# A gated mix of linear attention and a gated MLP on one core: first down weights loaded ahead of the gate weights, another order of low parts and gated additions at the end

## The chip, the cores and the metric

The kernel runs on one core of a Trainium2 chip. The metric is the device time of one execution in microseconds (us). Engines: PE multiplies matrices into PSUM, DVE and POOL do elementwise work, ACT does activations and copies, SP issues most DMAs. Each works through its own instructions in order, and waits on semaphores where it needs another's result.

## The reference

With `x` of 2048 tokens by 576:

```python
g = _sigmoid((x * gate_w).sum(-1, keepdims=True))
a = _A_ref(x, A_wqkv, A_wo)          # linear attention, 32 heads of 18, then @ wo
b = _B_ref(x, B_w_gate, B_w_up, B_w_down)
return g * a + (1 - g) * b
# _B_ref:
h = _gelu(x @ w_gate) * (x @ w_up)   # 576 -> 4608
return h @ w_down                    # 4608 -> 576
```

Everything is float32.

## The kernel before, in words

A float32 factor is split into a high part, which PE takes in one pass (`F32R`), and a low part, which is the rest; a product is three matmuls (high by high, high by low, low by high). ACT copies the high part, and DVE or POOL subtracts it for the low part.

The attention part comes first (lines 98 to 752). What is used of it here: `r2` holds the query features of one block of 512 tokens; `kw` holds the weights of the mixing product (`mixed`, L716), whose results, scaled by `g`, go to DRAM as `ga_d`. Its last `rb` loads are issued by SP at L695.

The MLP works in 36 periods. Each takes 256 of the 4608 features for one half of the tokens (1024); 18 periods do the first half, 18 the second. All products of a period are done by a scheme with seven half-size products for a 2 x 2 block product (`PRODUCTS`, L36), so sums of blocks are formed ahead (`S1` to `S4` of the left factor, `T1` to `T4` of the weights) and results are combined behind.

- Gate and up products `G1` to `G7`, `U1` to `U7` (`product`, L767): seven matmuls of 512 columns each, into four PSUM banks `bk`. DVE combines them (`gu2`, `ge3`, `uu2` and so on, all through the helper at L794), ACT applies the gelu (`gel0` to `gel3`, L791) in the tiles `e0` to `e3`; `um0` to `um3` make the four blocks of `h`.
- Down products `D20` to `D71` (`unit`, L870) of the period before, in 14 half units of six matmuls of 288 columns, into two PSUM pairs `pr`. DVE adds each (`E20` to `E71`, L879) to `sums`, which holds one half of the output.
- The left factors: `h11`, `h12`, `h22` and the sums `S1` to `S4`, each with a high copy on ACT (names in h, L917) and a low part on DVE or POOL (names in l, L918). `s1`, `s2`, `s3`, `s4` form the sums themselves; `S3` is made from `s3` alone. They lie in the tiles `h0` to `h3` and `hx0` to `hx2`.
- Down weights: `dld` loads `draw` (576 KB, L936); `dsT1` to `dsT4` form the sums in `dsum` on POOL and DVE; `dhr` and `dht` copy high parts to `wd` on ACT; `dlr0`, `dlr1`, `dlt0`, `dlt1` are low parts (L942). Gate and up weights of the first half go the same way from `work` (`wld0`, `wld1`, then `ws...`, `whr`, `wlr`, `wht`, `wlt`) to `wg` and `wu`; the second half loads them ready-made.

The order of a period's steps is written out by hand in `ORDER` (L38): it is recorded step by step by `emit`, and each engine's queue is what falls to it from that list. `@` puts a step on POOL instead of DVE, `+1` makes it belong to the period before. `tables` holds variants for three periods; that of the last, `LAST`, moves four steps ahead of `D10` and turns the order of the down products (what stands as `D10` becomes `D70`, which reads `S3`).

All tiles of the MLP are placed one behind the other in one pool, over tiles of the attention part that are done by then. A tile waits for the last instructions that used the memory beneath it. Before, `draw` begins in the memory of `kw`, with `dsum` behind it, and `e1` to `e3` lie in that of `r2`.

After the last period there are only its own down products. `parts(i)` (L1074) copies the high part of block `i` of `h` on ACT and notes its low part; `low_parts` (L1069) records the noted ones on DVE, one call later. `last_weights` (L1080) splits the last down weights, with two low parts on POOL (L1083). `down` (L1087) computes 128 tokens at a time, twelve matmuls a tile; `down_out` multiplies by `1 - g` and adds the sums (L1104, or by column halves at L1102), and SP stores the tile. Ahead of that, each tile of `sums` is scaled by `1 - g` on ACT and `ga_d`'s rows, loaded to `work` and `xu`, are added on POOL (`gated`, L863); for tiles whose sums are complete it is recorded behind the `G` and `U` steps.

Of the kernel before, what the change touches and what calls it, by code (L numbers as in the profile page):

```python
# [8 lines left out]
F32 = mybir.dt.float32  # L9
# [7 lines left out]
NB, BS = 4, 512  # L17
# [32 lines left out]
def tile_gated_mix(ctx, tc, xt, xr, xs, wkv, wvt, wq, wo, wgu, wgt, wdn, cst, out):  # L50
    nc = tc.nc
# [14 lines left out]
    def f32(ap):  # L66
        return ap.bitcast(F32)
# [479 lines left out]
    turn = Scope()  # L547
# [230 lines left out]
    es = [e0]  # L778
    add, sub, mul = OP.add, OP.subtract, OP.mult
# [4 lines left out]
    def ps(m, role):  # L784
        return bk[PLACE[m][role]]

    def copy(o, i):
        nc.scalar.activation(o, i, AF.Copy)  # L788
# [4 lines left out]
    def tt(o, a, b, op):  # L793
        nc.vector.tensor_tensor(o, a, b, op)  # L794
# [8 lines left out]
    def first_after(k):  # L803
# [6 lines left out]
        else:  # L810
# [15 lines left out]
    mp = mlp.pool("mp")  # L826
    work = mp.tile([128, 4 * 1024], F32, name="work")
    wraw, tsum = ([work[:, i * 1024:(i + 1) * 1024].rearrange("p (i k c) -> p i k c", i=4, k=2) for i in r]
                  for r in ((0, 1), (2, 3)))
    draw, dsum = (mp.tile([128, 4, 288], F32, name=x) for x in ("draw", "dsum"))  # L830
    es += [mp.tile([128, BS], F32, name=f"e{i}") for i in range(1, 4)]
    hs = [mp.tile([128, 2, BS], F32R, name=f"h{i}") for i in range(4)]
    hx = [mp.tile([128, 2, BS], F32R, name=f"hx{i}") for i in range(3)]
    hb = {A11: hs[0], A12: hs[1], A22: hs[3], S3: hs[2], S1: hx[0], S2: hx[1], S4: hx[2]}
# [5 lines left out]
    LAST = NQD - 1  # L840
# [4 lines left out]
    def feature(n):  # L845
        return n if n < NF2 else LAST - n

    def mix_of(t):
        return work[:, t * D:(t + 1) * D] if t < 7 else xu.rearrange("p a c -> p (a c)")[:, :D]
# [4 lines left out]
    def halves(t):  # L854
        return t.rearrange("p (n c) -> p n c", n=2)

    def acc_of(t):
        return sums[:, 0:2, t] if t < 4 else sums[:, 2:4, t - 4]

    def out_of(st):  # L860
        return halves(out[st * 128:(st + 1) * 128, :])

    def gated(p, t):  # L863
        st, m = p * PER + t, halves(mix_of(t))
        nc.scalar.activation(acc_of(t), acc_of(t), AF.Copy, scale=gate[:, 1, st:st + 1])
        nc.gpsimd.tensor_tensor(acc_of(t) if p else m, acc_of(t), m, add)
        if p == 0:
            nc.sync.dma_start(out_of(st), m)

    def unit(k, q):  # L870
# [67 lines left out]
    for x, i, src in (("r", slice(0, 3), draw[:, 1:4]), ("t", slice(3, 7), dsum)):  # L938
        op(f"dh{x}", lambda n, e, i=i, src=src: copy(wd[:, i, 0], src))
        for j in range(2):  # L940
            c = slice(j * 144, (j + 1) * 144)
# [8 lines left out]
    def w_load(n, m):  # L950
        nc.sync.dma_start(f32(W[m]), wp_d[feature(n)][m])

    for m in range(2):
# [6 lines left out]
        for j in range(2):  # L960
            i, o = slice(2 * j, 2 * j + 2), slice(3 + 2 * j, 5 + 2 * j)
# [35 lines left out]
    def valid(name, n):  # L997
        if name[0] == "w":
            return 1 <= n < NF2 - name.startswith("wst")
        if name[0] == "x":  # L1000
            return 2 <= n < 14
        if name[0] == "d":
            return 0 <= n < LAST and n != NF2
        return 0 <= n < LAST + (name[0] in "GUgu")
# [8 lines left out]
    def before(t, a, b):  # L1013
        w = [x for x in t if x[0] == a][0]
        t = [x for x in t if x[0] != a]
        t.insert([x[0] for x in t].index(b), w)
        return t
# [1 line left out]
    turned = {1: "7", 6: "4", 5: "1", 3: "6", 7: "5", 4: "3", 2: "2"}  # L1019
    tables = {0: before(table, "U4", "U3"), NF2: before(table, "G4", "G2")}  # L1020
    last = table
    for name in ("dlt0", "dlt1", "S3h", "S3l"):
        last = before(last, name, "D10")
    tables[LAST] = [(x[0] + turned[int(x[1])] + x[2:], s, e) if x[0] in "DE" and s == 1 else (x, s, e)
                    for x, s, e in last]
    last_of = [[name for name, _, _ in table if name[0] == g][-1] for g in "GU"]
# [4 lines left out]
    after = deque()  # L1031

    def emit(name, n, e):
        if (name, n) in done or not valid(name, n):
            return
        assert not (after and name[0] == "E" and n % NF2 == 0 and CHAINS[int(name[1])][1] in (C21, C22))
        done.add((name, n))
        ops[name](n, e)
        if name[0] in "GU":
            if after:  # L1040
                gated(*after.popleft())
            if n == NF2 - 1 and name[0] == "U":
                a = PRODUCTS[int(name[1])][0]
                nc.sync.dma_start(f32(xo[:, a]), xop_d[:, a])
            m = "GU".index(name[0])
            if name == last_of[m] and NF2 <= n < LAST:
                w_load(n + 1, m)
        if n in (NF2 - 1, LAST - 1):
            for t in range(PER):
                key = (n // NF2, t)  # L1050
                if key not in called and all((f"E{k}{t % 4 // 2}", n) in done for k in ENDS[t // 4]):
                    called.add(key)
                    after.append(key)

    for m in range(2):
        emit(f"wld{m}", 1, None)
    for p in range(-1, LAST):
        if p == LAST - 1:
            for t in range(PER):
                mix_load(1, t)  # L1060
        if p == NF2:
            for t in range(PER):
                mix_load(0, t)
        for name, shift, e in tables.get(p, table):
            emit(name, p - shift, e)

    lows = []

    def low_parts():  # L1069
        for i, src in lows:  # L1070
            tt(hs[i][:, 1], src, f32(hs[i][:, 0]), sub)
        lows.clear()

    def parts(i):  # L1074
        low_parts()
        src = es[i] if i in (0, 3) else ps(1, "d" if i == 1 else "e")
        copy(hs[i][:, 0], src)
        lows.append((i, src))

    def last_weights():  # L1080
        copy(wd[:, :4, 0], draw)
        for c in (slice(0, 144), slice(144, 288)):
            nc.gpsimd.tensor_tensor(wd[:, :4, 1, c], draw[:, :, c], f32(wd[:, :4, 0, c]), sub)  # L1083

    place = {}

    def down(t, f, turn, by_halves):  # L1087
        if f == 1:
            place[t] = ([ps(1, "c")[:, :288], ps(1, "a")[:, :288]] if t == 6 else
                        [pr[turn % 2][:, i, :288] for i in range(2)])  # L1090
        y = place[t]
        h, c = hs[(0 if t < 4 else 2) + f], slice((t % 4) * 128, (t % 4 + 1) * 128)
        for k, (a, wl) in enumerate(((0, 0), (0, 1), (1, 0))):
            for i in range(2):
                nc.tensor.matmul(y[i], h[:, a, c], wd[:, (1 - i, 2 + i)[f], wl], start=f == 1 and k == 0,  # L1095
                                 stop=f == 0 and k == 2, skip_group_check=True)

    def down_out(t, turn, by_halves):
        a, st, y = acc_of(t), PER + t, place[t]
        if t == 6 or by_halves:  # L1100
            for i in range(2):
                nc.vector.scalar_tensor_tensor(a[:, i], y[i], gate[:, 1, st:st + 1], a[:, i], op0=mul, op1=add)  # L1102
        else:
            nc.vector.scalar_tensor_tensor(a, pr[turn % 2][:, :, :288], gate[:, 1, st:st + 1], a, op0=mul, op1=add)  # L1104
        if by_halves:
            for i in range(2):
                nc.sync.dma_start(out_of(st)[:, i], a[:, i])
        else:
            nc.sync.dma_start(out_of(st), a)

    left = {name for name, _, _ in table if name[0] in "dD" and (name, LAST - 1) not in done}
    for p in (LAST, LAST + 1):
        for name, shift, e in tables.get(p, table):
            n = p - shift
            fresh = (name, n) not in done
            emit(name, n, e)
            if n == LAST and name in ("um0", "um1", "um2", "um3") and fresh:
                parts(int(name[2]))
            if n == LAST - 1 and name in left:
                left.discard(name)  # L1120
                if name[0] == "d" and not any(x[0] == "d" for x in left):
                    nc.sync.dma_start(draw, wdn[feature(LAST)])
                if not left:
                    last_weights()
    order = (0, 1, 2, 3, 4, 5, 6, 7) if last_of[1] in ("U4", "U7") else (4, 5, 6, 7, 0, 1, 2, 3)
    turns = {t: k - (k > order.index(6)) for k, t in enumerate(order)}
    low_parts()
    while after:
        gated(*after.popleft())
    for group in (order[:2],) + tuple((t,) for t in order[2:]):  # L1130
        for f in (1, 0):
            for t in group:
                down(t, f, turns[t], t == order[-1])
        for t in group:
            down_out(t, turns[t], t == order[-1])
    mlp.close()
    base.close()
    fixed.close()
# [60 lines left out]
```

## Time and profile before

| | |
|---|---|
| median of 3 runs | 1505.3 us (1504.97 to 1505.55) |
| the profiled execution | 1505.87 us, of which its span from the first to the last instruction 1504.1 us |
| PE busy | 1488.0 us (99%) |
| DVE, POOL, ACT busy | 1126.8, 758.5, 580.2 us |
| mean granted clock of PE | 0.999 |

A timeline row shows the start in us from the span's start, the duration in us, the engine and line, the operation, the tiles it writes and reads, the count of merged instructions, and in brackets how long the engine had been idle and what ended that. Matmuls overlap, and their ends are modelled, so a row of matmuls is best read by the distance from its start to the next row's start. A row of the chain of waits shows start, duration and what held the chain in that time.

### The profile page before, as it was taken

What the parts mean: (1) busy time and instruction counts of PE and PEld (TensorE: products, weight loads), DVE (VectorE), ACT (ScalarE), POOL (GpSimd) and SP (SyncE); (2) the same over time, 40 slices, a digit from 0 to 9 for tenths busy, and PEclk for the clock granted to TensorE, in tenths of its full rate; (3) what the DMA queues carried; (4) which work ended last, traced back from release to release, by engine and by line L of the source; (5) the groups of instructions that cost most, each with busy time, mean ns of one, the idle gap of its engine ahead of it and who ended that gap; (6) DMA issues with size and microseconds to landing.
All of it is one profiled execution on the core that took longest, in us unless ns stands there. A gap on an engine that the chain in (4) does not pass through costs nothing.

```text
span 1504.1 us, 21831 instructions
## 1 busy us (share of the span) xinstructions
PE 1488.0 (99%) x8332; PEld 1320.2 (88%) x8332; DVE 1126.8 (75%) x1722; ACT 580.2 (39%) x952; POOL 758.5 (50%) x716
## 2 busy tenths in 40 slices
PE   8999999999999999999999999999999999999998
PEld 7999889888888888888888888888888888888887
DVE  6675676488878888888788777776777777777766
ACT  6676755334334433434333323323222222222223
POOL 3763312377887787887776634323322323323323
PEclk9999999999999999999999999999999999999999
DMA  6898537556677667666666385444333433444531
GB/s 201 275 350 308 152 124 228 184 195 222 242 250 242 217 213 239 208 203 236 231 230 210 89 347 183 147 179 166 139 139 146 180 151 139 153 182 157 200 139 63
DMA packets 118582, 295.60 MB, mean 197 GB/s; under 512 B 7181, under 2 KB 87245, under 8 KB 108110
## 3 DMA queue, kind: packets, MB, share of 16 engines
q1 hardware_dynamic: 114730, 281.04, 53.1%
q10 hardware_dynamic: 3380, 10.78, 2.0%
q0 software_dynamic: 368, 2.39, 0.5%
q8 instruction: 65, 1.06, 0.3%
q14 instruction: 39, 0.32, 0.1%
HBM read 181.51 MB, written 112.68 MB: 196 GB/s over the span
## 4 chain that ended last, share of the span: by engine, by line
PE 92%; POOL 2%; DMA 2%; DVE 1%; issue 1%; ACT 1%; SPq 1%; DVEq 0%; POOLq 0%
PE bank L775 52%; PE pair L876 26%; PE pair L716 4%; PE bank L483 3%; PE kp L218 2%; PE ms L259 1%; PE mp L259 1%; PE bank L486 1%; PE pair L1095 1%; PE den L658 1%; POOL work L934 1%; DMA row_raw<-xr 0%; DMA draw<-wdn 0%; DMA raw<-wgu 0%; DMA xr<-xt 0%
## 5 line engine op out<-in xcount | busy, mean ns | idle before, releaser
L794 DVE TENSOR_TENSOR sums<-pair,sums 128x576 f32<-128x576 f32 x474 | 354.8, 755 | 163.9 <-PE pair L876 152.1
L775 PE MATMUL bank<-xo,wg 128*128 128x512 f32 x1764 | 441.1, 393 | 1.2 <-POOL wg L962 1.2
L775 PE MATMUL bank<-xo,wu 128*128 128x512 f32 x1764 | 430.4, 393 | 1.0 <-DVE spare L794 1.0
L775 PEld LDWEIGHTS bank<-xo,wu 128*128 128x128 f32 x1764 | 323.6, 188 | 64.7 <-DVE spare L794 1.6
L775 PEld LDWEIGHTS bank<-xo,wg 128*128 128x128 f32 x1764 | 322.7, 189 | 60.4 <-POOL wg L962 1.9
L876 PEld LDWEIGHTS pair<-wd,h 128*128 128x128 f32 x1680 | 248.4, 189 | 20.0 <-ACT h L788 1.6
L876 PE MATMUL pair<-wd,h 128*128 128x288 f32 x1680 | 259.9, 297 | 2.0 <-ACT h L788 1.2
L794 DVE TENSOR_TENSOR spare<-bank,spare 128x512 f32<-128x512 f32 x216 | 148.3, 687 | 84.6 <-PE bank L775 69.2
L876 PEld LDWEIGHTS pair<-wd,hx 128*128 128x128 f32 x1260 | 179.1, 189 | 9.6 <-POOL hx L918 0.3
L876 PE MATMUL pair<-wd,hx 128*128 128x288 f32 x1260 | 184.7, 295 | 0.1
L788 ACT ACTIVATE spare<-bank 128x512 f32<-128x512 f32 x72 | 43.2, 600 | 353.5 <-PE bank L775 353.5
L918 POOL TENSOR_TENSOR h<-e,h 128x512 fp32r<-128x512 f32 x70 | 96.9, 1384 | 146.7 <-ACT h L788 146.7
L942 POOL TENSOR_TENSOR wd<-draw,wd 128x432 fp32r<-128x432 f32 x68 | 75.1, 1125 | 189.4 <-ACT wd L788 189.4
L934 POOL TENSOR_TENSOR work<-work 128x256 f32<-128x256 f32 x136 | 114.8, 854 | 5.3
L788 ACT ACTIVATE h<-e 128x512 fp32r<-128x512 f32 x71 | 44.4, 625 | 170.3 <-DVE e L794 170.3
L918 POOL TENSOR_TENSOR hx<-spare,hx 128x512 fp32r<-128x512 f32 x35 | 45.8, 1309 | 109.1 <-ACT hx L788 109.1
L794 DVE TENSOR_TENSOR e<-bank,spare 128x512 f32<-128x512 f32 x107 | 73.2, 684 | 8.2 <-PE bank L775 6.9
L788 ACT ACTIVATE wd<-draw 128x864 fp32r<-128x864 f32 (+1 forms) x35 | 32.7, 934 | 113.0 <-PE pair L876 110.5
L791 ACT ACTIVATE e<-e 128x512 f32<-128x512 f32 x108 | 65.5, 622 | 0.1
L942 POOL TENSOR_TENSOR wd<-dsum,wd 128x576 fp32r<-128x576 f32 x34 | 49.3, 1451 | 24.5 <-ACT wd L788 24.5
L716 PEld LDWEIGHTS pair<-kw,p 128*128 128x128 f32 x448 | 60.5, 189 | 0.7
L716 PE MATMUL pair<-kw,p 128*128 128x288 f32 x448 | 60.9, 295 | 0.0
(200 smaller groups left out, 1898.3 us busy)
## 6 DMA issues: line engine op xcount, KB each, us to landing
wg<-wp_d SPq DMA_DIRECT2D x17, 2240.0 KB
wu<-wp_d SPq DMA_DIRECT2D x17, 2240.0 KB
wp_d<-wg SPq DMA_DIRECT2D x16, 2240.0 KB
wp_d<-wu SPq DMA_DIRECT2D x16, 2240.0 KB
draw<-wdn SPq DMA_DIRECT2D x35, 576.0 KB
work<-wgu SPq DMA_DIRECT2D x34, 512.0 KB
xo<-xop_d SPq DMA_DIRECT2D x7, 1280.0 KB
wt_d<-tail_op SPq DMA_DIRECT2D x15, 448.0 KB
```

The source lines that it names most:

```text
L218: nc.tensor.matmul(ps[c][:, :n], xa, kvw[i][:rows, r, lo:lo + n], start=(k == 0), stop=(k == 13))
L259: nc.tensor.matmul(o, a, p[:, w, lo:lo + n], start=(t == 0 and i == 0 and first), stop=(t == NST - 1 and i == len(ops) - 1), skip_group_ch ...
L483: nc.tensor.matmul(ps, qw[i][:rows, c:c + 128], xa, start=(k == 0), stop=(k == 13))
L716: nc.tensor.matmul(y[:, i, :288], pa, w[:, i * 288:(i + 1) * 288], start=(n == 0), stop=(n == 13))
L775: nc.tensor.matmul(ps, w_, x_, start=start and i == 0, stop=i == 6, skip_group_check=not start)
L788: nc.scalar.activation(o, i, AF.Copy)
L791: nc.scalar.activation(o, i, AF.Gelu_apprx_tanh)
L794: nc.vector.tensor_tensor(o, a, b, op)
L876: nc.tensor.matmul(pr[q][:, j, :288], h[:, hl, c], wd[:, b, wl], start=start and i == 0, stop=i == 2, skip_group_check=not start)
L918: op(name + "l", lambda n, e, a=a, f=src_of: e.tensor_tensor(hb[a][:, 1], f(), f32(hb[a][:, 0]), sub))
L934: op(f"{name}T{i + 1}", lambda n, e, o=o, a=a, b=b: e.tensor_tensor(o, a, b, sub))
L942: op(f"dl{x}{j}", lambda n, e, i=i, src=src, c=c: e.tensor_tensor(wd[:, i, 1, c], src[:, :, c], f32(wd[:, i, 0, c]), sub))
```

## The change

It has five parts.

1. `dld` of period 0 is recorded ahead of `wld0` and `wld1`. For this the tiles `e1` to `e3` are placed ahead of `draw`, with a filler `gap` of 512 bytes a partition behind them: `draw` now begins where `r2` begins, and `e1` to `e3` lie over `kw`. All tiles behind lie 512 bytes further.
2. In the last period `S3h` moves ahead of `s1`; `S3l` and `dlt0` move ahead of `s2`, and `S3l` from POOL to DVE; `dlt1` stays at its place in `ORDER`.
3. Behind the last period's `um2` the low part of block 3 goes to POOL; the low parts of blocks 2, 1 and 0 follow on DVE, in this order, after `um0`.
4. `gated` of the second half of the tokens only notes its POOL addition in `added`; those noted are recorded behind the low part of block 3, the others after the last low parts. No `gated` is recorded behind the very last `U` product.
5. The last tiles are done in the order 6, 7, 4, 5, 0, 1, 2, 3, not 4, 5, 6, 7, 0, 1, 2, 3; the third goes to the two single banks. The last does all six matmuls of its first 288 columns, then those of the second, each in a bank of its own.

SP at the start of the loop, before (`rb` belongs to the attention part, `wgu` holds the raw gate and up weights, `wt_d` a part of the split ones):

```order
L695 DMA rb_2907<-rden_d11_66 128x1x256 x4
L695 DMA rb_2907<-rden_d11_66 64x1x256 x2
L955 DMA work_3270<-wgu 128x4x256 x2
L936 DMA draw_3271<-wdn 128x1152
L947 DMA wg_2874<-wt_d0_126 96x7x128
```

and after:

```order
L695 DMA rb_2907<-rden_d11_66 128x1x256 x4
L695 DMA rb_2907<-rden_d11_66 64x1x256 x2
L941 DMA draw_3275<-wdn 128x1152
L960 DMA work_3270<-wgu 128x4x256 x2
L952 DMA wg_2874<-wt_d0_126 96x7x128
```

The load of `draw` has passed the two loads of `work`. It waits for ACT's and DVE's last reading of `r2`; the first load of `work` waits for the last matmul on `kw`, as before.

DVE in the last period, before (`e2` holds `s3`; `e3` becomes `s1`, `spare` `s2`, `e1` `s4`; the rows of `sums` are `E20` and `E21`):

```order
L794 TENSOR_TENSOR e3_3275<-bank_3261,e3_3275 128x512
L794 TENSOR_TENSOR sums_3284<-pair_3265,sums_3284 128x576
L921 TENSOR_TENSOR spare_1924<-e3_3275,spare_1924 128x512
L794 TENSOR_TENSOR e1_3273<-bank_3264,spare_1924 128x512
L942 TENSOR_TENSOR wd_3283<-dsum_3272,wd_3283 128x4x144
L794 TENSOR_TENSOR sums_3284<-pair_3266,sums_3284 128x576
```

and after:

```order
L794 TENSOR_TENSOR e3_3273<-bank_3261,e3_3273 128x512
L794 TENSOR_TENSOR sums_3285<-pair_3265,sums_3285 128x576
L923 TENSOR_TENSOR h2_3279<-e2_3272,h2_3279 128x512
L947 TENSOR_TENSOR wd_3284<-dsum_3276,wd_3284 128x4x144
L926 TENSOR_TENSOR spare_1924<-e3_3273,spare_1924 128x512
L794 TENSOR_TENSOR e1_3271<-bank_3264,spare_1924 128x512
L794 TENSOR_TENSOR sums_3285<-pair_3266,sums_3285 128x576
```

The low part `S3l` (into `h2`) is new on DVE, and `dlt0` has passed `s2` and `s4`. On ACT the copy `h2<-e2` has passed the copies `hx0<-e3` and `spare<-bank`.

DVE after the last `U` products, before (bank 3264 is block 1 of `h`, bank 3261 block 2, `e3` block 3, `spare` block 0):

```order
L794 TENSOR_TENSOR bank_3264<-bank_3264,e1_3273 128x512
L794 TENSOR_TENSOR h3_3279<-e3_3275,h3_3279 128x512
L794 TENSOR_TENSOR bank_3261<-spare_1924,bank_3261 128x512
L794 TENSOR_TENSOR bank_3261<-bank_3261,e2_3274 128x512
L794 TENSOR_TENSOR h1_3277<-bank_3264,h1_3277 128x512
L794 TENSOR_TENSOR spare_1924<-bank_3263,spare_1924 128x512
L794 TENSOR_TENSOR h2_3278<-bank_3261,h2_3278 128x512
L794 TENSOR_TENSOR h0_3276<-spare_1924,h0_3276 128x512
```

and after:

```order
L794 TENSOR_TENSOR bank_3264<-bank_3264,e1_3271 128x512
L794 TENSOR_TENSOR bank_3261<-spare_1924,bank_3261 128x512
L794 TENSOR_TENSOR bank_3261<-bank_3261,e2_3272 128x512
L794 TENSOR_TENSOR spare_1924<-bank_3263,spare_1924 128x512
L1076 TENSOR_TENSOR h2_3279<-bank_3261,h2_3279 128x512
L1076 TENSOR_TENSOR h1_3278<-bank_3264,h1_3278 128x512
L1076 TENSOR_TENSOR h0_3277<-spare_1924,h0_3277 128x512
```

The low part into `h3` is gone from DVE; on POOL it stands behind the two low parts of the last weights and ahead of the eight additions into `sums`. The other three stand behind all sums.

The diff, without the layout lines told above and without `lows.clear()` and what it replaces:

```diff
@@ gated
+    added = deque()
+
     def gated(p, t):
         st, m = p * PER + t, halves(mix_of(t))
         nc.scalar.activation(acc_of(t), acc_of(t), AF.Copy, scale=gate[:, 1, st:st + 1])
-        nc.gpsimd.tensor_tensor(acc_of(t) if p else m, acc_of(t), m, add)
-        if p == 0:
+        if p:
+            added.append(lambda: nc.gpsimd.tensor_tensor(acc_of(t), acc_of(t), m, add))
+        else:
+            nc.gpsimd.tensor_tensor(m, acc_of(t), m, add)
             nc.sync.dma_start(out_of(st), m)
@@ tables
-    for name in ("dlt0", "dlt1", "S3h", "S3l"):
-        last = before(last, name, "D10")
+    for name, at in (("S3h", "s1"), ("S3l", "s2"), ("dlt0", "s2")):
+        last = before(last, name, at)
+    last = [(x, s, nc.vector if x == "S3l" else e) for x, s, e in last]
@@ emit
-            if after:
+            if after and (n < LAST or name != last_of[1]):
                 gated(*after.popleft())
@@ the loop's start
-    for m in range(2):
-        emit(f"wld{m}", 1, None)
+    for name, n in (("dld", 0), ("wld0", 1), ("wld1", 1)):
+        emit(name, n, None)
@@ the last period
                 parts(int(name[2]))
+                if name == "um2":
+                    low_part(*lows.pop(0), nc.gpsimd)
+                    while added:
+                        added.popleft()()
@@ the end
-    order = (0, 1, 2, 3, 4, 5, 6, 7) if last_of[1] in ("U4", "U7") else (4, 5, 6, 7, 0, 1, 2, 3)
+    order = (6, 7, 4, 5, 0, 1, 2, 3)
-    low_parts()
+    for i, src in sorted(lows, reverse=True):
+        low_part(i, src, nc.vector)
     while after:
         gated(*after.popleft())
-    for group in (order[:2],) + tuple((t,) for t in order[2:]):
+    while added:
+        added.popleft()()
+    for group in (order[:2],) + tuple((t,) for t in order[2:-1]):
...
+    for i in range(2):
+        for f in (1, 0):
+            down(order[-1], f, 0, True, (i,))
+    down_out(order[-1], 0, True)
```

More of the change, by code (lines that the diff above doesn't have):

```diff
@@ L829, in tile_gated_mix @@
                   for r in ((0, 1), (2, 3)))
+    es += [mp.tile([128, BS], F32, name=f"e{i}") for i in range(1, 4)]
+    mp.tile([128, 128], F32, name="gap")
     draw, dsum = (mp.tile([128, 4, 288], F32, name=x) for x in ("draw", "dsum"))
-    es += [mp.tile([128, BS], F32, name=f"e{i}") for i in range(1, 4)]
     hs = [mp.tile([128, 2, BS], F32R, name=f"h{i}") for i in range(4)]
@@ L1067, in tile_gated_mix, with low_part @@
     lows = []
[L1069 to L1072, printed above, removed]
+    def low_part(i, src, e):
+        e.tensor_tensor(hs[i][:, 1], src, f32(hs[i][:, 0]), sub)
     def parts(i):
-        low_parts()
         src = es[i] if i in (0, 3) else ps(1, "d" if i == 1 else "e")
@@ L1085, in tile_gated_mix, with down @@
     place = {}
-    def down(t, f, turn, by_halves):
+    def down(t, f, turn, by_halves, halves_too=(0, 1)):
         if f == 1:
-            place[t] = ([ps(1, "c")[:, :288], ps(1, "a")[:, :288]] if t == 6 else
+            place[t] = ([ps(1, "c")[:, :288], ps(1, "a")[:, :288]] if t == order[2] or by_halves else
                         [pr[turn % 2][:, i, :288] for i in range(2)])
@@ L1093, in down @@
         for k, (a, wl) in enumerate(((0, 0), (0, 1), (1, 0))):
-            for i in range(2):
+            for i in halves_too:
                 nc.tensor.matmul(y[i], h[:, a, c], wd[:, (1 - i, 2 + i)[f], wl], start=f == 1 and k == 0,
@@ L1099, in down_out @@
         a, st, y = acc_of(t), PER + t, place[t]
-        if t == 6 or by_halves:
+        if t == order[2] or by_halves:
             for i in range(2):
@@ L1124, in tile_gated_mix @@
                     last_weights()
-    order = (0, 1, 2, 3, 4, 5, 6, 7) if last_of[1] in ("U4", "U7") else (4, 5, 6, 7, 0, 1, 2, 3)
-    turns = {t: k - (k > order.index(6)) for k, t in enumerate(order)}
-    low_parts()
+    order = (6, 7, 4, 5, 0, 1, 2, 3)
+    turns = {t: k - (k > 2) for k, t in enumerate(order)}
+    for i, src in sorted(lows, reverse=True):
+        low_part(i, src, nc.vector)
     while after:
         gated(*after.popleft())
-    for group in (order[:2],) + tuple((t,) for t in order[2:]):
+    while added:
+        added.popleft()()
+    for group in (order[:2],) + tuple((t,) for t in order[2:-1]):
         for f in (1, 0):
             for t in group:
-                down(t, f, turns[t], t == order[-1])
+                down(t, f, turns[t], False)
         for t in group:
-            down_out(t, turns[t], t == order[-1])
+            down_out(t, turns[t], False)
+    for i in range(2):
+        for f in (1, 0):
+            down(order[-1], f, 0, True, (i,))
+    down_out(order[-1], 0, True)
     mlp.close()
```

## The prediction

> **What bounds the kernel now.** The chain of waits came first; it gives PE's pace.
>
> ```profile
> 327.51 1.59 PE pair L876 x12
> 329.10 6.45 PE bank L775 x28
> ```
>
> Undisturbed, 28 matmuls of 512 columns take 6.45 us, 0.230 each, and 12 of 288 columns 1.59, 0.1325 each. PE is on almost the whole chain, so the time falls only where its matmuls start later than this pace. Inside the loop PE keeps it; the timeline shows three places where it doesn't: the start of the loop, the last period, the end. First the start.
>
> ```profile
> 286.95 5.15 PE L775 MATMUL bank<-xo,wu 128*128 128x512 f32 x21
> 293.14 5.09 PE L775 MATMUL bank<-xo,wu 128*128 128x512 f32 x21 [1.04 <-DVE spare L794]
> 298.07 0.63 PE L775 MATMUL bank<-xo,wg 128*128 128x512 f32 x2
> ```
> ```profile
> 312.50 2.13 PE L876 MATMUL pair<-wd,hx 128*128 128x288 f32 x12
> 314.47 1.79 PE L775 MATMUL bank<-xo,wu 128*128 128x512 f32 x7
> ```
> ```profile
> 299.89 1.42 PE L775 MATMUL bank<-xo,wg 128*128 128x512 f32 x5 [1.19 <-POOL wg L962]
> ```
>
> 21 matmuls from 286.95 last to 291.78, yet the next starts at 293.14: 1.36 lost. 21 more end at 297.97 (0.10 lost), two end at 298.53, the third starts at 299.89: 1.36. Twelve from 312.50 should end at 314.09; the next starts at 314.47: 0.38. Together 3.20. The other engines say why (POOL, then ACT, then SP, whose rows are DMA issues):
>
> ```profile
> 291.05 2.39 POOL L942 TENSOR_TENSOR wd<-draw,wd 128x432 fp32r<-128x432 f32 x2
> 293.40 3.40 POOL L934 TENSOR_TENSOR work<-work 128x256 f32<-128x256 f32 x4
> 296.76 1.84 POOL L958 TENSOR_TENSOR wg<-work,wg 128x768 fp32r<-128x768 f32 x1
> 298.57 1.27 POOL L962 TENSOR_TENSOR wg<-work,wg 128x512 fp32r<-128x512 f32 x1
> 299.80 1.29 POOL L918 TENSOR_TENSOR h<-e,h 128x512 fp32r<-128x512 f32 x1
> ```
> ```profile
> 289.15 0.93 ACT L788 ACTIVATE wd<-draw 128x864 fp32r<-128x864 f32 x1 [2.50 <-DMA draw<-wdn]
> ```
> ```profile
> 253.72 9.69 SPq L695 DMA_DIRECT2D rb<-rden_d  x12
> 280.73 1.27 SPq L955 DMA_DIRECT2D work<-wgu  x2
> 282.05 0.70 SPq L936 DMA_DIRECT2D draw<-wdn  x1
> ```
>
> `draw`, the first down weights, is issued last of three, at 282.05, and ACT sits idle 2.50 us until it lands. POOL's queue runs on from it without a pause to the low part of the gate weights (298.57 + 1.27 = 299.84), for which PE waits until 299.89. DVE has two of the sums of `draw` in its queue ahead of the addition that frees the bank that PE waits for at 291.78.
>
> **The first load.** It moves ahead of both gate loads on SP. Its tile now lies on `r2` and not on `kw`, so it waits no longer for the last matmul on `kw` (280.7), but for the last reader of `r2`:
>
> ```profile
> 259.88 0.29 DVE L706 TENSOR_TENSOR p<-r,p 64x128 fp32r<-64x128 f32 x1
> ```
>
> This ends at 260.17, before SP is through with its `rb` loads (253.72 + 9.69 = 263.41); the new wait adds nothing. Behind it stand the two `work` loads, which wait for 280.7 as before. `e1` to `e3` lie on `kw` instead; they are first written from a product that PE starts after the last matmul on `kw`, so that wait is free. So `draw` leaves at about 263.5 and has 23 us, where it had 7. ACT can then start its copy 2.50 us earlier, at 286.65, and end at 287.58; POOL's low parts, which follow it, start at 287.6 instead of 291.05 and everything behind them shifts by 3.4. The gate weights' low part is ready at 296.4. PE, with its first 1.36 gone, reaches the matmul that needs it at 298.53 - 1.36 - 0.10 = 297.07: no wait. By the second place PE is 2.8 earlier and POOL 3.4, so the 0.38 goes too. Bounds: 1.36 if POOL gains nothing, 3.4 with two gaps of a tenth that I leave out. I take 3.2. The gate loads are no longer shared with `draw` and land no later.
>
> **The last period.** PE, a window with its mean granted clock (the 0.57), ACT and DVE:
>
> ```profile
> 1452.81 1.76 PE L775 MATMUL bank<-xo,wg 128*128 128x512 f32 x7
> 1455.77 0.53 PE L876 MATMUL pair<-wd,h 128*128 128x288 f32 x2 [1.20 <-ACT h L788]
> 1457.12 1.16 PE L876 MATMUL pair<-wd,h 128*128 128x288 f32 x4 [0.82 <-POOL h L918]
> 1458.08 3.01 PE L775 MATMUL bank<-xo,wg 128*128 128x512 f32 x7
> 1460.93 0.96 PE L876 MATMUL pair<-wd,h 128*128 128x288 f32 x6
> ```
> ```profile
> 1457.00:1461.00 4.00, 3.88 (x12) 3.25 (x13) 0.00 (x0) 0.00 (x0) 2.53 (x3) 0.57 0.03 11
> ```
> ```profile
> 1454.60 0.60 ACT L788 ACTIVATE spare<-bank 128x512 f32<-128x512 f32 x1 [2.89 <-PE bank L775]
> 1455.09 0.62 ACT L788 ACTIVATE h<-e 128x512 fp32r<-128x512 f32 x1
> ```
> ```profile
> 1452.34 0.69 DVE L794 TENSOR_TENSOR e<-bank,spare 128x512 f32<-128x512 f32 x1
> 1452.95 0.75 DVE L942 TENSOR_TENSOR wd<-dsum,wd 128x576 fp32r<-128x576 f32 x1
> ```
>
> The seven from 1452.81 end at 1454.42. The first down product (with `S3`) starts at 1455.77, 1.35 late, since its high part stands on ACT behind a copy of PE's own result; two matmuls later it waits for the low part on POOL, 1456.04 to 1457.12, 1.08. Then four take 0.96 instead of 0.53 and seven 2.85 instead of 1.61, at a mean clock of 0.57: 1.67. In all 4.10.
>
> The change puts the high part ahead of `s1`, behind work that ACT has done by 1452 (it is idle 2.89 before 1454.60), and the low part and one part of the weights (0.75) on DVE ahead of `s2` and `s4`. Before, `s4` ends at 1453.03; with 0.69 and 0.75 put ahead it ends near 1454.5. The built program gives PE one new wait: the product after the first half of the down product starts after `s4`, which reads its bank. Without stalls that is 1454.42 + 0.80 = 1455.2: 0.7 to spare. Behind it PE would hold everything; if DVE were late by more, that excess is the price. So 4.1 goes; between 2.4 (clock unchanged) and 4.1.
>
> [...]
>
> **The end.** PE, then DVE, then POOL:
>
> ```profile
> 1485.88 1.75 PE L1095 MATMUL pair<-wd,h 128*128 128x288 f32 x12
> 1488.03 0.79 PE L1095 MATMUL pair<-wd,h 128*128 128x288 f32 x4 [0.40 <-ACT h L788]
> 1489.18 1.33 PE L1095 MATMUL pair<-wd,h 128*128 128x288 f32 x8 [0.37 <-DVE h L794]
> ```
> ```profile
> 1484.28 1.66 DVE L794 TENSOR_TENSOR h<-e,h 128x512 fp32r<-128x512 f32 x1
> ...
> 1500.13 0.94 DVE L1102 SCALAR_TENSOR_TENSOR sums<-pair,gate,sums 128x288 f32<-128x288 f32 x2 [0.77 <-PE pair L1095]
> ```
> ```profile
> 1482.55 2.84 POOL L1083 TENSOR_TENSOR wd<-draw,wd 128x576 fp32r<-128x576 f32 x2 [23.02 <-issue]
> ...
> 1488.56 8.84 POOL L866 TENSOR_TENSOR sums<-sums,work 128x576 f32<-128x576 f32 x6
> ```
>
> PE loses 1488.03 - 1487.47 = 0.56 and 1489.18 - 1488.56 = 0.62, 1.18 in all, since DVE's low part of `h3` (1.66) stands ahead of the sums for `h2`. That part moves to POOL, behind the weights (1482.55 + 2.84 = 1485.39), and takes 1.29 (the row at 299.80), so it is ready at 1486.7. PE wants it at its fifth matmul, 1485.88 + 0.53 = 1486.41: a new wait of 0.3. With the 1.66 gone DVE makes the two sums for `h2` (0.69 each, by the row at 1452.34) from 1484.4 to about 1486.0 with the hand-overs, then one more sum and `h2`'s low part by about 1487.5; PE wants that after 16 matmuls, at 1488.3. The third gated scaling, which ACT no longer has ahead of its copy for `h2`, is work that POOL's additions want only later. Gain 1.18 - 0.3 = 0.9; if POOL's low part took DVE's 1.66, 0.5; if it cost nothing, 1.2.
>
> [...]
>
> POOL's eight additions, 8.84 / 6 = 1.47 each, now start 1.3 later, at 1486.7, and end at 1498.5. PE's eight tiles of 1.59 end at 1485.88 + 0.3 + 12.7 = 1498.9. The last addition is needed by then: 0.4 to spare.
>
> Of the last tile's two output operations (0.94), the first runs under the second half's six matmuls (0.8), so 0.45 goes; 0 if the last store waits for the earlier one anyway. The matmuls are as many as before.
>
> **The sum.** 3.2 + 4.1 + 0.9 + 0.45 = 8.65 us off the profiled execution, which took 1505.87 (its span 1504.1 and 1.8 around it). That is 0.6 above the runs' median of 1505.3; the difference goes onto the median: 1496.7.
>
> **Rivals.**
>
> 1. The early load buys nothing: POOL or DVE, held by something that the trace does not separate from the load, lets PE wait in the same places. Against it speaks ACT's idle 2.50 for the load and nothing else. 5.45 remains: 1499.9.
> 2. The low clock is not the stall's doing and stays. For it: PE was not idle throughout, and the two losses of 1.36 at the start brought no slow matmuls behind them (21 in 4.93 from 293.14). Against it: the slow matmuls stand right behind the longest wait of the three places. 1.67 less: 1498.3. [...]
> 3. The end passes to POOL. Should each addition take 1.8 instead of 1.47 beside the busier DVE, eight end 2.6 later and the last output waits 2.2: 1498.9. It decides from 1.52 on. Against it: six of them ran at 1.47 with the same outputs beside them.
> 4. Slower. All tiles behind `draw` lie 512 bytes or more elsewhere in SBUF; should that cost in each of the 34 later periods, 0.25 us a period eats the gain and 0.34 makes it 3 us slower, 1508.3. With 84 down matmuls a period that is 4 ns on each of them. Against it, means of matmuls that read tiles in different places:
>
> ```profile
> L876 PE MATMUL pair<-wd,h 128*128 128x288 f32 x1680 | 259.9, 297 | 2.0 <-ACT h L788 1.2
> ...
> L876 PE MATMUL pair<-wd,hx 128*128 128x288 f32 x1260 | 184.7, 295 | 0.1
> ```
>
> They differ by 2 ns: at most 84 x 34 x 2 ns = 5.7 us.
>
> 5. The change doesn't do what it says: the steps move but a neighbour on the same queue stops PE as long, at all three places. 1505.
>
> **How the numbers follow.** Forecast 0.74, rivals 0.09, 0.07, 0.05, 0.02, 0.03. The range goes from the upper bounds (3.4 + 4.1 + 1.2 + 0.45 = 9.15, and half a microsecond for what an earlier finish brings the last stores: 1495.7) to rival 1: 1499.9. A measurement of this kernel tells about 0.2%, 3 us, from no change; the forecast and rivals 1 to 3 lie beyond it. Faster 0.95, same 0.03, slower 0.02.
>
> **What would show it.** In the new trace `draw` is issued near 263, ACT's copy of it has no wait for a DMA, and 42 matmuls run from 287 at one pace. In the last period there is no gap ahead of the first down product and no stretch of low clock; if the stretch stays without a gap, rival 2 holds. At the end there is one gap, of about 0.3, with POOL's low part as releaser. A gain below 3 us, or a longer period in the loop, would prove me wrong.

## The result and the profile after

| | before | after |
|---|---|---|
| median of 6 runs each | 1505.47 us (1504.97 to 1506.55) | 1497.58 us (1496.44 to 1498.25) |
| after to before | | 0.9947, 95% interval 0.9934 to 0.9960 |
| the profiled execution, its span | 1505.87, 1504.1 | 1498.25, 1496.4 |

The change is 7.9 us faster (6.0 to 9.9 by the interval). The forecast was 1496.7, within 1495.7 to 1499.9.

To see where it came from, cut the span by PE's rows into six pieces: up to the first fourteen gate matmuls of the loop (280.50 before, 281.17 after); from there to the first up product behind the first down product that reads `hx` (the start); to the first `G6` of the last period (the loop); to the first of the final down matmuls (the last period); to the end of PE's last matmul, which is the start of its last row and 0.1325 for each matmul of that row (the end); and the tail to the end of the span.

| us | before | after | gain | forecast |
|---|---|---|---|---|
| up to the loop | 280.50 | 281.17 | -0.67 | 0 |
| the start | 33.97 | 30.99 | 2.98 | 3.2 |
| the loop | 1133.51 | 1133.46 | 0.05 | 0 |
| the last period | 37.90 | 33.76 | 4.14 | 4.1 |
| the end | 14.00 | 13.09 | 0.91 | 0.9 |
| the tail | 4.22 | 3.93 | 0.29 | 0.45 |
| the span | 1504.1 | 1496.4 | 7.70 | 8.65 |

**The start.** SP, ACT and POOL in the profile after:

```profile
265.28 0.34 SPq L941 DMA_DIRECT2D draw<-wdn  x1
281.40 1.26 SPq L960 DMA_DIRECT2D work<-wgu  x2
```
```profile
287.21 0.91 ACT L788 ACTIVATE wd<-draw 128x864 fp32r<-128x864 f32 x1
```
```profile
268.70 0.81 POOL L939 TENSOR_TENSOR dsum<-draw 128x288 f32<-128x288 f32 x1 [10.69 <-DMA draw<-wdn]
...
295.85 1.29 POOL L967 TENSOR_TENSOR wg<-work,wg 128x512 fp32r<-128x512 f32 x1
```

`draw` leaves at 265.28, not at 282.05, and POOL reads it 3.4 us later. ACT's copy has no bracket any more: it is not idle before it. POOL's low part of the gate weights ends at 297.14, where it ended at 299.84. And PE:

```profile
287.61 9.84 PE L775 MATMUL bank<-xo,wu 128*128 128x512 f32 x42
297.29 1.78 PE L775 MATMUL bank<-xo,wg 128*128 128x512 f32 x7
298.91 0.97 PE L881 MATMUL pair<-wd,h 128*128 128x288 f32 x6
299.99 1.89 PE L775 MATMUL bank<-xo,wg 128*128 128x512 f32 x7
301.72 0.97 PE L881 MATMUL pair<-wd,h 128*128 128x288 f32 x6
```

42 matmuls run in one row, and the next starts 9.68 later, 0.2305 each: both losses of 1.36 are gone. What is left stands behind: six matmuls from 298.91 should end at 299.71, and the next product starts at 299.99 (0.28 lost); seven from there end at 301.60, the next start at 301.72 (0.12). That 0.12 goes with the first loss: the second matmul behind the wait starts at 300.33, 0.34 after the first, where the pace is 0.23. DVE's row shows the first one's reason, the sum `um0` that frees the bank, done at 299.93:

```profile
299.25 0.68 DVE L794 TENSOR_TENSOR spare<-bank,spare 128x512 f32<-128x512 f32 x1
```

**The last period.** PE, then ACT and DVE, of after:

```profile
1450.45 1.76 PE L775 MATMUL bank<-xo,wg 128*128 128x512 f32 x7
1452.05 0.97 PE L881 MATMUL pair<-wd,h 128*128 128x288 f32 x6
1452.86 1.76 PE L775 MATMUL bank<-xo,wg 128*128 128x512 f32 x7
```
```profile
1447.51 0.63 ACT L788 ACTIVATE h<-e 128x512 fp32r<-128x512 f32 x1
```
```profile
1451.26 0.69 DVE L794 TENSOR_TENSOR e<-bank,spare 128x512 f32<-128x512 f32 x1
```

Every row of PE starts where the one before ends by the pace (1450.45 + 7 x 0.2304 = 1452.06, + 6 x 0.1325 = 1452.85): no gap, no slow matmul. ACT has made the high part of `S3` at 1448.1, 4 us ahead of its reader at 1452.05. `s4`, the DVE row, behind the two operations that now stand ahead of it, ends at 1451.95; the product that now waits for it starts at 1452.86, so 0.9 is to spare where 0.7 was reckoned.

**The end and the tail.** PE, then POOL, then DVE:

```profile
1479.38 3.73 PE L1098 MATMUL pair<-wd,h 128*128 128x288 f32 x24
1482.95 1.75 PE L1098 MATMUL bank<-wd,h 128*128 128x288 f32 x12
1484.53 6.51 PE L1098 MATMUL pair<-wd,h 128*128 128x288 f32 x48
1490.88 1.78 PE L1098 MATMUL bank<-wd,h 128*128 128x288 f32 x12
```
```profile
1478.84 1.30 POOL L1076 TENSOR_TENSOR h<-e,h 128x512 fp32r<-128x512 f32 x1
1480.08 1.46 POOL L870 TENSOR_TENSOR sums<-sums,work 128x576 f32<-128x576 f32 x1
1481.48 1.91 POOL L870 TENSOR_TENSOR sums<-sums,xu 128x576 f32<-128x576 f32 x1
1483.34 8.37 POOL L870 TENSOR_TENSOR sums<-sums,work 128x576 f32<-128x576 f32 x6
```
```profile
1492.70 0.52 DVE L1105 SCALAR_TENSOR_TENSOR sums<-bank,gate,sums 128x288 f32<-128x288 f32 x1 [0.23 <-PE bank L1098]
```

The first 24 matmuls take 3.57 to the next row where the pace gives 3.18: 0.39 lost, while POOL's low part, which they need, ends at 1480.14 (the fifth matmul would start at 1479.91). The eight additions end at 1491.71, ahead of PE's last matmul at 1492.47. DVE's last half ends at 1493.22, 0.75 behind that; before, the two halves ended 1.19 behind it (1501.07 against 1499.88).

### The profile page after: what moved, and what is told of

Read it like the earlier page. It is cut to its first block, busy times and chain, and to the rows that moved or that the text cites. A ratio compares the mean times of both kernels' runs of the same rounds, so it can differ in the third digit from the quotient of the medians.

```text
span 1496.4 us, 21832 instructions
## 1 busy us (share of the span) xinstructions
PE 1485.8 (99%) x8332; PEld 1320.4 (88%) x8332; DVE 1126.8 (75%) x1722; ACT 580.6 (39%) x952; POOL 757.3 (51%) x716
## 4 chain that ended last, share of the span: by engine, by line
PE 95%; DMA 2%; ACT 1%; DVE 1%; POOL 1%; issue 0%; SPq 0%; DVEq 0%
PE bank L775 54%; PE pair L881 26%; PE pair L716 4%; PE bank L483 3%; PE kp L218 2%; PE ms L259 1%; PE mp L259 1%; DMA xr<-xt 1%; PE bank L486 1%; PE pair L1098 1%; PE den L658 1%; DMA row_raw<-xr 1%; DMA raw<-wgu 0%; PE pair L615 0%; ACT row_op L229 0%
```

## The experiments

The theory: three stalls of PE, each with an own cause in the queue of one other engine, go independently of each other, and the low clock behind the second goes with it. The rivals tried are that the gain of the start needs the new place in memory, that the other tiles' new places cost or bring something, that the last period needs all of its moves, and that the low clock is not the stall's doing. Each trace is cut into the six pieces of above; the pieces that an edit doesn't touch serve as its control.

| us | up to the loop | start | loop | last period | end | tail |
|---|---|---|---|---|---|---|
| before | 280.50 | 33.97 | 1133.51 | 37.90 | 14.00 | 4.22 |
| start_alone | 281.23 | 30.97 | 1133.37 | 37.89 | 13.98 | 4.26 |
| order_alone | 280.89 | 30.99 | 1133.39 | 37.87 | 13.98 | 4.28 |
| layout_alone | 281.46 | 33.94 | 1133.50 | 36.32 | 14.00 | 4.18 |
| last_alone | 280.83 | 34.08 | 1133.36 | 33.76 | 14.01 | 4.26 |
| s3h_alone | 280.47 | 33.68 | 1133.45 | 33.76 | 14.00 | 4.24 |
| end_alone | 281.82 | 33.86 | 1133.38 | 36.30 | 13.11 | 4.23 |
| tile_alone | 280.43 | 33.75 | 1133.40 | 37.77 | 13.98 | 3.97 |
| after | 281.17 | 30.99 | 1133.46 | 33.76 | 13.09 | 3.93 |
| two_more | 280.73 | 30.89 | 1133.40 | 33.76 | 12.71 | 4.01 |

**Part 1 whole (start_alone)**: the kernel before with

```diff
-    draw, dsum = (mp.tile([128, 4, 288], F32, name=x) for x in ("draw", "dsum"))
...
+    mp.tile([128, 128], F32, name="gap")
+    draw, dsum = (mp.tile([128, 4, 288], F32, name=x) for x in ("draw", "dsum"))
...
-    for m in range(2):
-        emit(f"wld{m}", 1, None)
+    for name, n in (("dld", 0), ("wld0", 1), ("wld1", 1)):
+        emit(name, n, None)
```

> Only the first part of the change: the tiles e1 to e3 ahead of draw, and the first load of draw ahead of the gate loads. Theory (three separate seams, each with its own waits): the stretch from the loop's first product to the U product behind the first S2 product (33.97 us before, 30.99 with the whole change) shrinks to about 31.0; the last period keeps its two waits and the half clock, the end its gaps; about 3.0 us faster than before. Rival (the seams are linked, a finish earlier at the start is given back at the next wait for a transfer): under 1.5 us faster.

Measured: 1502.83 us (10 runs, 1501.47 to 1503.98) beside 1505.54 of before; ratio 0.9980 (0.9971 to 0.9990). The start takes 30.97; the pieces behind it are as before, and the stretch up to the loop, which the edit does not touch, is 0.73 longer (that is taken up at the end of the next section).

**The order without the new places (order_alone)**: only the second half of that diff.

> Only the order of issue: the first load of draw ahead of the gate loads, but over the old memory, so that it waits for the last matmul on kw as the gate loads do. Theory A (what counts is to be first of the three): draw, issued near 281, lands within 3.5 to 4.5 us, by 285.5, before ACT wants it at 286.7; the first stretch takes at most 31.5 us, gain 2.5 to 3.0 us. Theory B (what counts is the early release through the new place): draw still lands too late, near 288; the first stretch takes 33 us or more, gain under 1 us.

Measured: 1502.22 us; ratio 0.9979 (0.9970 to 0.9989); the start takes 30.99. SP and POOL:

```profile
281.12 0.34 SPq L936 DMA_DIRECT2D draw<-wdn  x1
281.51 1.26 SPq L955 DMA_DIRECT2D work<-wgu  x2
```
```profile
285.27 0.99 POOL L934 TENSOR_TENSOR dsum<-draw 128x288 f32<-128x288 f32 x1 [27.54 <-DMA draw<-wdn]
```

`draw` still waits for the last matmul on `kw` and leaves at 281.12, 16 us later than in after. But now it is first of the three, and POOL has it after 4.15 us; before, ACT waited for it until 289.15, 7.1 behind its issue at 282.05. That is early enough: the whole 2.98 comes from being first in SP's queue, and nothing from the new place.

**The new places without the order (layout_alone)**: only the first half of that diff.

> Only the new places of the tiles; the first load of draw stays third in SP's queue. Theory A: SP's queue is in order, so draw is issued near 282 as before; the first stretch takes 33.9 us, no change in the time (within 0.5 us). Theory B: at least 1.5 us of the gain comes without the new order. The slower rival of the prediction (tiles in other places cost in each period): the 33.76 us of a period of the loop grow by 0.1 us or more, 3 us in all.

Measured: 1505.21 us; ratio 0.9999 (0.9990 to 1.0008). The loop takes 1133.50 against 1133.51, so in this trace tiles in other places cost nothing in 34 periods. The last period of its trace is 1.58 shorter than that of before, though nothing in it was changed; that is taken up below.

**Part 2 whole (last_alone)**: the kernel before with the diff of `tables` shown above.

> Only the second part of the change: S3h ahead of s1, S3l on DVE and dlt0 ahead of s2 in the last period. Theory: the last period, from its first gate product to the first product of the last tiles (37.90 us before, 33.76 with the whole change), takes 33.8, without low clock; 4.1 us faster. Rival (the low clock is not the wait's doing): it takes 35.4, with a stretch of half clock, 2.4 us faster.

Measured: 1501.91 us (10 runs, 1501.09 to 1502.09) beside 1505.47; ratio 0.9976 (0.9967 to 0.9985). The last period takes 33.76, as in after.

**Only ACT's copy moved (s3h_alone)**:

```diff
-    for name in ("dlt0", "dlt1", "S3h", "S3l"):
-        last = before(last, name, "D10")
+    for name, at in (("dlt0", "D10"), ("dlt1", "D10"), ("S3l", "D10"), ("S3h", "s1")):
+        last = before(last, name, at)
```

> Of the second part only the high part S3h ahead of s1 on ACT; S3l stays on POOL and dlt0 and dlt1 stay ahead of the first turned product, as before. Theory: the one cause of both waits was ACT's queue, where S3h stood behind the copy of PE's product; POOL is idle and makes S3l by about 1452, so the last period takes 33.8 us as with the whole second part, 4.1 us faster. Rival (POOL's low part needs its move to DVE): PE still waits for POOL, at least 0.5 us, and the period takes 34.3 or more.

Measured: 1501.54 us; ratio 0.9976 (0.9966 to 0.9985), the last period again 33.76. ACT's rows tell why:

```profile
1449.49 0.63 ACT L788 ACTIVATE h<-e 128x512 fp32r<-128x512 f32 x1
1450.70 0.63 ACT L788 ACTIVATE hx<-e 128x512 fp32r<-128x512 f32 x1 [0.58 <-DVE e L794]
1454.23 0.60 ACT L788 ACTIVATE spare<-bank 128x512 f32<-128x512 f32 x1 [2.89 <-PE bank L775]
```

With its high part 5 us earlier, the low part on POOL is early too. `S3l` on DVE and the new place of `dlt0` were not needed; one step on one queue makes the whole gain. In the medians that is 3.9 us, where last_alone has 3.6; intervals of 0.0009 to either side (1.4 us) do not tell the two apart, nor either from the 4.1 expected.

**Parts 3 and 4 and the order of the tiles (end_alone)**: after's `added`, `low_part`, the low part of block 3 on POOL and the order 6, 7, 4, 5, 0, 1, 2, 3, but the last tile as before.

> Only the parts at the end but for the last tile's halves: low part of block 3 on POOL, the others behind the sums on DVE, gated additions noted and recorded later, tile order 6, 7, 4, 5, 0 to 3. Theory: from the first product of the last tiles to PE's last matmul 13.1 us instead of 14.0, 0.9 us faster, and POOL's additions end before the last output operation. Rival: PE gains at the head, but the last output operations wait for POOL's additions, which gives back 0.5 us or more.

Measured: 1504.54 us; ratio 0.9996 (0.9987 to 1.0005), which alone can't be told from no change. The end takes 13.11, 0.89 less; the tail 4.23, as before.

**The last tile by column halves (tile_alone)**:

```diff
-    for group in (order[:2],) + tuple((t,) for t in order[2:]):
+    for group in (order[:2],) + tuple((t,) for t in order[2:-1]):
...
+    for i in range(2):
+        for f in (1, 0):
+            down(order[-1], f, 0, True, (i,))
+    down_out(order[-1], 0, True)
```

> Only the last tile by column halves, in two banks. Theory: one of the two last output operations runs beside the second half's matmuls, so from PE's last matmul to the end of the span 3.8 us instead of 4.2, 0.3 to 0.45 us faster. Rival: the end is set by the last store's transfer, which starts no earlier; under 0.15 us.

Measured: 1504.54 us; ratio 0.9997 (0.9987 to 1.0006), again not to be told from no change; the tail takes 3.97, 0.25 less, a little under the 0.3 to 0.45 expected. The four ratios of the parts (order, last, end, tile) multiplied give 0.9948; the whole measured 0.9947. The parts add up, as far as ratios with such intervals can show it; the table of pieces shows it place by place.

**How long PE must wait for the low clock (clock_holds)**: after, with fills of a tile that nothing reads (0.48 us each) on DVE ahead of `um1`: 4 in period 21, two more in every second period, up to 16 in period 33. Nothing is left out.

```diff
+    idle = mp.tile([128, 512], F32, name="idle")
+    HOLDS = {21: 4, 23: 6, 25: 8, 27: 10, 29: 12, 31: 14, 33: 16}
...
+            if name == "um1":
+                for _ in range(HOLDS.get(p, 0)):
+                    nc.vector.memset(idle, 0.0)
```

> The changed kernel with 4, 6, 8, 10, 12, 14 and 16 extra fills of an unused tile on DVE ahead of um1 in seven periods of the second half (21, 23, ... 33), so that PE waits there for a time that grows from about 0 to some 6 us; otherwise the whole computation. Theory (the half clock is the answer to a wait of PE): the granted clock falls to 0.5 for about 3.4 us behind the longer waits, from a wait of 2 to 3 us on, and not behind those under 1.5 us; each fall costs about 1.7 us more than the wait. Rival (the fall in the last period had another cause): PE's clock stays at 1.0 behind waits of 2 to 4 us.

Measured: 1542.56 us (one run). PE's rows at the first two places, then windows at the first four, whose column ahead of the last two is the granted clock:

```profile
1008.78 0.43 PE L883 MATMUL pair<-wd,h 128*128 128x288 f32 x2
1009.41 0.80 PE L883 MATMUL pair<-wd,h 128*128 128x288 f32 x4 [0.20 <-DVE h L925]
1010.60 1.89 PE L775 MATMUL bank<-xo,wg 128*128 128x512 f32 x7 [0.40 <-DVE spare L794]
...
1075.83 1.77 PE L775 MATMUL bank<-xo,wg 128*128 128x512 f32 x7
1078.66 0.53 PE L883 MATMUL pair<-wd,h 128*128 128x288 f32 x2 [1.06 <-ACT h L788]
1079.39 0.80 PE L883 MATMUL pair<-wd,h 128*128 128x288 f32 x4 [0.20 <-DVE h L925]
1080.58 2.91 PE L775 MATMUL bank<-xo,wg 128*128 128x512 f32 x7 [0.39 <-DVE spare L794]
```
```profile
1006.00:1012.00 6.00, 5.41 (x25) 4.12 (x24) 5.54 (x11) 2.29 (x3) 1.42 (x1) 1.00 0.65 227
1081.20:1084.40 3.20, 3.20 (x11) 2.72 (x10) 3.17 (x6) 0.63 (x1) 0.00 (x0) 0.50 0.92 383
1152.90:1156.10 3.20, 2.94 (x8) 2.12 (x7) 3.17 (x6) 1.26 (x2) 1.17 (x1) 0.50 0.91 381
1224.60:1231.20 6.60, 5.72 (x16) 4.63 (x17) 6.46 (x11) 2.91 (x4) 1.42 (x1) 0.50 0.62 260
```

By the pace, PE loses 1.03 us at the first place (from 1008.78 to 1010.60, less six matmuls of 0.1325), and the clock stays at 1.00. At the second it loses 2.35 (the seven from 1075.83 end at 1077.44, the next seven start at 1080.58, and six of 0.1325 lie between), and the clock falls to 0.50. The brackets add up to less, 0.60 and 1.65, since they go by modelled ends. From the trace's record of the granted clock: the low stretches last 3.41, 3.41, 6.83, 6.83, 6.83 and 10.24 us, that is one, two or three times 3.413, and their starts (1081.13, 1152.81, 1224.49, 1299.58, ...) lie whole multiples of 3.413 apart (71.68 is 21 times). So all of them fit one grid of 3.413 us through this trace, with waits of different lengths between them. The records of the profiled pair fit such a grid too: before has half clock from 1457.35 to 1460.76 (3.41) and again from 1505.13, 14 times 3.413 behind 1457.35; after has it from 18.97 to 22.38 (3.41) and again from 1496.94, 433 times 3.4133 behind 18.97; the second stretch of each lies behind the span's end. One step of a trace's grid is called a window here. With the time in each window that had a matmul at its full pace counted as busy, in this trace a window that was busy 0.36 or less was followed by a window of half clock, and one that was busy 0.77 was not. These shares are estimates from PE's rows: the profile's own busy time, which goes by modelled ends, is 1.39 of the 3.42 us from 1453.93 to 1457.35 in before, where the count gives 0.26.

**The same stall, cut or not by a window's edge.** Six of the profiled kernels have the stall of before in their last period, row for row, with waits of 1.20 and 0.82. Four of them have the low clock behind it, layout_alone and end_alone have not. PE of layout_alone, then its window behind the stall:

```profile
1456.69 0.53 PE L877 MATMUL pair<-wd,h 128*128 128x288 f32 x2 [1.20 <-ACT h L788]
1458.04 0.80 PE L877 MATMUL pair<-wd,h 128*128 128x288 f32 x4 [0.82 <-POOL h L919]
1458.68 1.78 PE L775 MATMUL bank<-xo,wg 128*128 128x512 f32 x7
1460.30 0.97 PE L877 MATMUL pair<-wd,h 128*128 128x288 f32 x6
```
```profile
1460.00:1464.00 4.00, 4.00 (x21) 3.42 (x21) 2.02 (x3) 0.00 (x0) 0.48 (x1) 1.00 0.00 0
```

The seven from 1458.68 take 1.62; those from 1458.08 in before took 2.85. By the pace the stall takes 2.55 here (from 1455.34, where the product ahead of it ends, to 1458.68, less six of 0.1325), more than the 2.35 that brought the low clock in clock_holds. Where the windows lie is worked out, in steps of 3.413, from a low stretch elsewhere in the same trace:

| | busy share of the window(s) that hold the stall | clock behind it | last period, us |
|---|---|---|---|
| order_alone | 0.25 | half | 37.87 |
| before | 0.26 | half | 37.90 |
| start_alone | 0.29 | half | 37.89 |
| tile_alone | 0.35 | half | 37.77 |
| layout_alone | 0.80, 0.45 | full | 36.32 |
| end_alone | 0.55, 0.71 | full | 36.30 |

In clock_holds and these six traces the shares with half clock behind them end at 0.36, and those without begin at 0.45. Counted in the same way, the windows with a wait of 2.69 us in the attention part (its rows stand in the next section) lie closer together: in after, layout_alone and last_alone that window was about 0.42 busy and half clock followed, in tile_alone 0.45 and none did. With half clock behind it the stall costs 4.0 to 4.1 (37.77 to 37.90 less the 33.76 of after), without it 2.55; the mean of the six is 3.6. Each of these kernels has one trace, so that the outcome changes between executions of one and the same kernel is not shown at this place directly. The runs carry a trace of it, though one that low stretches elsewhere, in the attention part above all, blur: of the 65 runs of before made beside the experiments 21 had a mean clock of 0.997 or less (on average 1506.16 us) and 37 one of 0.999 or more (1504.89); of the 31 runs of last_alone, s3h_alone, after and two_more, which don't have the stall, none was at 0.997.

**What was left (two_more)**: after, with `um0` ahead of `um2` in the first period, for the 0.28 lost ahead of 299.99, and the low part of block 3 used last in both of the first two tiles, for the 0.39.

```diff
-    tables = {0: before(table, "U4", "U3"), NF2: before(table, "G4", "G2")}
+    tables = {0: before(before(table, "U4", "U3"), "um0", "um2"), NF2: before(table, "G4", "G2")}
...
+            for ks in ((0, 1), (2,)) if len(group) == 2 and f else ((0, 1, 2),):
+                for t in group:
+                    down(t, f, turns[t], False, parts_of=ks)
```

> The changed kernel with two more steps against the waits that it has left: in the first period um0 ahead of um2, so that the bank of G7 comes free earlier; and in the first two of the last tiles the low part of block 3 as the last product of both tiles, so that POOL has 0.53 us more for it. Theory: PE's two remaining waits (0.3 to 0.4 us at each place) go: the first stretch 30.6 us instead of 30.99, the end 12.7 instead of 13.09; 0.8 us faster than the changed kernel, 8.5 to 9 faster than before. Rival (another neighbour holds PE there as long): under 0.3 us less in the two stretches together.

Measured: 1496.96 us (5 runs, 1496.41 to 1497.74); ratio to before 0.9946 (0.9932 to 0.9959), where after had 0.9947: no difference that these runs can tell. In the trace:

```profile
298.47 0.97 PE L881 MATMUL pair<-wd,h 128*128 128x288 f32 x6
299.28 1.76 PE L775 MATMUL bank<-xo,wg 128*128 128x512 f32 x7
300.88 0.97 PE L881 MATMUL pair<-wd,h 128*128 128x288 f32 x6
301.87 1.88 PE L775 MATMUL bank<-xo,wg 128*128 128x512 f32 x7
...
1478.78 3.36 PE L1098 MATMUL pair<-wd,h 128*128 128x288 f32 x24
1481.97 1.75 PE L1098 MATMUL bank<-wd,h 128*128 128x288 f32 x12
```

The end lost its gap (3.19 from row to row, 0.38 gained, 12.71 as expected). At the start the gap only moved: 299.28 follows at the pace, but the product behind the next six starts at 301.87 where 301.68 was due, so of 0.28 only 0.10 is gained: the start takes 30.89 and not the 30.6 expected. What one sum gains by going first on DVE, the next one loses.

## Why the prediction was right

- **The start, forecast 3.2, measured 2.98.** The causes held: `draw` was late, POOL's queue ran on behind it, and both losses of 1.36 and the 0.38 are gone. The rest is 0.40 of new gaps (0.28 and 0.12) less the two gaps of a tenth that the forecast left out. That `draw` must leave early, by its new place, was an assumption too many; order_alone shows that first of three is enough. It left at 265.28, not near 263.5; with 20 us to spare this changed nothing. Rival 1, that the early load buys nothing, is refuted.
- **The last period, forecast 4.1, measured 4.14 in the profiled pair, 3.6 as the mean of the six traces with the stall.** In the runs' medians last_alone gains 3.6 and s3h_alone 3.9, which fit both. The causes held, and the waits of 1.35 and 1.08, 2.43 together, are there, as 2.55. What was mis-sized is the half clock: its 1.67 was taken as a cost of every execution, from a profile that happened to have it. Two of six profiled kernels with the same stall don't pay it, so that the profiled pair gives 4.14 is in part luck. Rival 2, that the low clock stays, would have given 1498.3, and 1497.58 lies about midway between that and the forecast; the traces refute it, not the time: the low clock appears in the last period of no trace of the four without the stall, and clock_holds brings it into the loop with waits alone.
- **The half clock.** The traces show it in stretches of 3.41, 6.83 and 10.24 us, on a grid of 3.413 in clock_holds, before and after, and with an outcome that differs between the six traces with the same stall. By the count, an estimate, the windows ahead of it were busy about 0.42 or less (0.26 in before), and of those counted at 0.45 or more none had it behind. So it came behind windows in which PE had worked for part of the time, and rival 2's support, that PE was not idle throughout, falls.
- **The end, forecast 0.9, measured 0.91 and, alone, 0.89.** POOL's low part took 1.30 (forecast 1.29) and left a gap of 0.39 (forecast 0.3). Rival 3, POOL's additions as the new bound, did not come: the first took 1.46, the second 1.91, the last six 1.40 each, together 11.6 from 1480.08, and they were done 0.8 us ahead of PE's last matmul.
- **The tail, forecast 0.45, measured 0.29 and, alone, 0.25.** DVE gained its 0.44 (1.19 to 0.75 behind PE's last matmul). But from DVE's end to the end of the span it now takes 3.18 and not 3.03, and the other 0.15 went there. All three kernels with halves have tails of 3.93 to 4.01, all seven with the whole tile 4.18 to 4.28. Why the store took longer was not tried.
- **Rival 4, slower by the tiles' places**, is refuted by layout_alone (ratio 0.9999; the loop within 0.15 us in every kernel). Rival 5 is refuted by the gain of each part in its own piece of the trace.

The sum: on the profile it was 8.65 and came to 8.32 in the four places, 0.22 short at the start and 0.16 in the tail. The profiled runs differ by only 7.70, since the run of after came to the loop 0.67 later, and the loop itself was 0.05 shorter. PE near the span's start, where it waits 2.69 us in both kernels, before and then after:

```profile
18.15 4.00 PE L218 MATMUL kp<-kvw,xo 128*128 128x288 f32 x28 [2.69 <-DVE zsum L246]
21.98 2.58 PE L259 MATMUL ms<-pk,row_op 128*128 128x320 f32 x18
```
```profile
17.46 5.50 PE L218 MATMUL kp<-kvw,xo 128*128 128x288 f32 x28 [2.69 <-DVE zsum L246]
22.80 2.57 PE L259 MATMUL ms<-pk,row_op 128*128 128x320 f32 x18
```

28 matmuls take 3.83 in the one and 5.34 in the other, which has a low stretch of 3.41 there: after comes to this place 0.69 earlier and leaves it 0.82 later. No edit reaches it. The clock is not all that varies there: end_alone, with a low stretch of 6.83, comes to the loop last of all, at 281.82, and tile_alone, without any, first, at 280.43, but s3h_alone with one of 3.41 is at 280.47. All these differences arise in the first 80 us, to within a tenth, and what else makes them was not looked into. In the medians the gain is 7.9. The forecast's 8.65, less 0.5 for the half clock that not every execution has and some 0.4 for the start and the tail, makes 7.75; with 6.0 to 9.9 as the interval that fits, but the medians don't test it finely.

## What to carry to other kernels

Look for the one step on an in-order queue that stands behind something it does not need: here one copy on ACT and one DMA issue on SP made 3.9 and 3.3 us when tried alone, of 7.9 in all, and the moves around them were not needed. Four of the six traces with the same stall had a stretch of half clock behind it, 1.6 us of its cost (37.90 against 36.32), and two had none: price such a stretch by how often several traces show it, and take the wait alone as the sure part. A gap of a few tenths that is closed by turning the order on a busy engine may only move to that engine's next result, as 0.18 of 0.28 us did in two_more.

## What the runs showed of the hardware

- Half clock came in stretches of 3.41, 6.83 and 10.24 us (clock_holds), whose starts lie whole multiples of 3.413 us apart (71.68 is 21 times); the stretch in before lasted 3.41 (1457.35 to 1460.76), that in after 3.41 (18.97 to 22.38). By the count from PE's rows, an estimate, the windows ahead of half clock were busy up to about 0.42, and those of 0.45 or more had none behind them. A loss of 2.35 us, in pieces with matmuls between, had half clock behind it in clock_holds; the 2.55 us of this kernel's stall had none in layout_alone, where by the count they lay across two windows (0.80 and 0.45 busy).
- Behind the wait of 2.69 us in the attention part, at 17 to 24 us, there was no low stretch in the traces of before and tile_alone, one of 3.41 us in the others but end_alone, which had 6.83; one of 3.41 costs 1.5 us there (28 matmuls take 5.34 in after and 3.83 in before). The mean clock of the runs of before (0.997 or less at 1506.16 us on average, 0.999 or more at 1504.89) suggests that executions of one and the same kernel differ in part by these two places.
- A load of 576 KB was read 3.4 us behind its issue where SP issued the next load 16 us later (after), 4.2 where it was issued first of three (order_alone), and 7.1 where it was issued behind two loads of 512 KB (before).
